# Loading q and k by 256 tokens in an attention and SwiGLU kernel on one Trainium2 core

## The chip, the cores and the metric

The kernel runs on one core of one Trainium2 chip. A core has five engines that run side by side, each working through its own list of instructions in order: TensorE (PE in the profile, with its weight loads as PEld), VectorE (DVE), ScalarE (ACT), GpSimd (POOL) and SyncE (SP). POOL and SP do no arithmetic here: they issue DMA transfers, which 16 DMA engines carry out. An instruction that waits for a semaphore holds up everything behind it on its own engine. The metric is device time in microseconds (us), the median of several runs.

## The reference

Inputs are q, k and v (8 batches, 8 heads, 576 tokens, 64 values a head, float32) and three weight matrices. The first half is causal attention over a sliding window of 128 tokens with an ALiBi bias, a slope for each head:

```python
scores = scale * np.matmul(q, k.transpose(0, 1, 3, 2))
rel = pos[:, None] - pos[None, :]
bias = slopes[:, None, None] * (-np.abs(rel).astype(np.float32))[None, :, :]
mask = (rel >= 0) & (rel < window)
scores = np.where(mask, scores + bias[None], -1000000000.0)
# softmax over the keys, then
np.matmul(attn, v)
```

Its output, 4608 tokens of 512 values, goes through a SwiGLU block without biases:

```python
g = x @ w_gate
silu = g * (1.0 / (1.0 + np.exp(-g)))
val = x @ w_val
return (silu * val @ w_out).astype(np.float32)
```

with 512 inputs, 1536 hidden values and 512 outputs.

## The kernel before

**Attention.** Two batches make a super-batch, and the 36 units of attention are 9 tiles of 128 tokens in each of 4 super-batches: four tiles of its first batch, four of its second, and one tile made of the last 64 tokens of both. Such a tile of q, k or v is called a rank, 0 to 35. For a unit, `scores` multiplies a rank's transposed k with the transposed q of this and the next rank (line 289; line 325 for a batch's last tiles), ACT takes the exponential (295, 329), DVE multiplies by a mask that holds the exponentials of the bias (301, 333), `weighted` multiplies by V with a column of ones beside it (357), and DVE divides by that column (360, 361). The result x is transposed into xT (385 to 389, for late units by a DMA, 379).

**Loading q, k and v.** POOL issues all loads from HBM that turn float32 into float16, in an order written out by hand at lines 917 to 955 and by `loads_to` afterwards, seven ranks ahead. A load of q or k (line 188) brings one rank as 128 tokens, 8 heads and 64 values: 1024 runs of 256 bytes in HBM, 128 bytes in SBUF. At most eight of POOL's loads are under way: each waits for the one eight places earlier.

**Transposing q and k.** Scores need both with the 64 values on the partitions. Ranks below `QK_DMA_FROM` = 11 are transposed by PE, four instructions a tile (215), and copied out of PSUM by DVE (220) or ACT (218). Later ranks are transposed by a DMA that SP issues (236), four units ahead (`ahead`). They land in `kT` and `qT`, rings of 12 and 9 ranks.

**The feed-forward part.** Tokens are taken in nine blocks of 512. For each of 12 slices of 128 hidden values, PE computes pg = w_gate·xT and pv = w_val·xT (413); ACT takes tanh into tt (431), DVE makes uu = (tt + 1)·pg (432) and hT = uu·pv (443). Three PSUM buffers called gv go round among pg and pv; for the first two slices of the first block four buffers of the other pool are used, the one that transposes and scores take too. Output projections follow (467 and, with seven products in place of eight, 548 to 590). Blocks 6 to 8 do the gate and value products by sevens as well (637). SP issues the stores (459), in line with its transposes.

**What sets the order.** The start, up to unit 4, and the first steps of `ffn` are written out in order for PE, DVE and ACT (`tc.manual_schedule`). In between, `everything` interleaves steps of `ffn` with steps of `attention` by a target count, and the framework's scheduler lays out the engines from a model of costs; from step 60 the order of PE is as written. On the chip each engine follows that fixed order.

Of the kernel before, what the change touches and what calls it, by code (L numbers as in the profile page):

```python
# [10 lines left out]
FP32 = mybir.dt.float32  # L11
# [5 lines left out]
P = 128  # L17
WIN = 128
QK_DMA_FROM = 11
X_DMA_FROM = 22  # L20
MASKS_AT = (3.0, 5.0, 6.0, 7.0)
# [22 lines left out]
def make_distance():  # L44

    u = np.arange(2 * P)[None, :] - np.arange(P)[:, None]
    return np.where((u >= 0) & (u < WIN), u, 16000).astype(np.float32)
# [3 lines left out]
def kernel(  # L51
# [25 lines left out]
    dist, idf = stage[:, 5, 0:256], stage[:, 5, 256:384]  # L77
    hw = {key: stage[:, n] for n, key in enumerate((("k", 0), ("q", 0)))}
# [9 lines left out]
    dist_d = nc.inline_tensor(make_distance(), name="distance")  # L88
    nc.scalar.dma_start(dist, dist_d.ap())

# [11 lines left out]
    def later_masks():  # L102
        for h in by_slot:
            nc.scalar.activation(reg[:, slot(h), :], dist, AF.Exp, scale=-(2.0 ** (-8.0 * (h + 1) / H)))


    NK, NQ = 12, 9
# [11 lines left out]

    def make_mask(n):  # L120
        to, of = ((msk[0][:, :, 0:64], reg[:, :, 128:192]),
                  (msk[1][:, :, 64:128], reg[:, :, 128:192]),
                  (msk[2][0:64, :, 0:64], reg[0:64, :, 0:64]),
                  (msk[2][64:128, :, 64:128], reg[64:128, :, 64:128]))[n]
        nc.scalar.copy(to, of)
# [8 lines left out]
    nat = ctx.enter_context(tc.tile_pool(name="nat", bufs=5))  # L134
# [16 lines left out]
    VROW = 80  # L151
# [7 lines left out]


    units = [(s, p) for s in range(NSUP) for p in range(9)]
    last = len(units) - 1
    NR = 9 * NSUP

    natq, natk, va = {}, {}, {}

    def transposed_home(name, rank):
        return kT[:, rank % NK] if name == "k" else qT[:, rank % NQ]

    def source(src, rank):  # L170

        s, c = divmod(rank, 9)
        if c == 8:
            return [((64 * n, 64 * n + 64),
                     src[2 * s + n, :, 512:576, :].rearrange("h p d -> p h d")) for n in range(2)]
        b, t = 2 * s + c // 4, c % 4
        return [((0, P), src[b, :, t * P:(t + 1) * P, :].rearrange("h p d -> p h d"))]

    def load_v(rank):
        va[rank] = va_all[rank % NV]  # L180
        for (p0, p1), src in source(v, rank):
            nc.gpsimd.dma_start(va[rank][p0:p1, :, 0:D], src)  # L182

    def load_qk(rank, which="kq"):
        for name in which:
            t_ = nat.tile([P, H, D], FP16, name=name + "n", tag=name + "n")
            for (p0, p1), src in source(k if name == "k" else q, rank):
                nc.gpsimd.dma_start(t_[p0:p1], src)  # L188
            (natk if name == "k" else natq)[rank] = t_

    def load(rank):
        load_qk(rank)
        load_v(rank)

    def transposed(name, rank):

        if rank < FIRST:
            pt = ps_f.tile([P, 4, P], FP32 if (name, rank) in hw else FP16, name="pt",
                           tag="gv" if name == "k" or rank == 1 else "po",
                           bufs=3 if name == "k" or rank == 1 else 1)  # L200
        else:
            pt = ps_a.tile([P, 4, P], FP16, name="pt", tag="a")
        if (name, rank) in hw:

            for _ in range(IDLE[(name, rank)]):
                nc.tensor.matmul(pt.rearrange("p j t -> p (j t)"), idle[:, 0:P], idle,
                                 start=True, stop=True)
            for j in range(4):
                nc.tensor.transpose(pt[:, j, :], hw[(name, rank)][:, j * P:(j + 1) * P], idf)
            nc.vector.tensor_copy(transposed_home(name, rank), pt)  # L210
            return
        t_ = (natk if name == "k" else natq).pop(rank)

        for j in range(4):
            nc.tensor.transpose(pt[:, j, :], t_[:, 2 * j:2 * j + 2, :],
                                idm if rank < FIRST else idm2)
        if name == "k" and rank >= FIRST:
            nc.scalar.copy(transposed_home(name, rank), pt)
        else:
            nc.vector.tensor_copy(transposed_home(name, rank), pt)  # L220


    order = []
    for s in range(NSUP):
        for half in (0, 4):
            order += [(name, 9 * s + half + r) for name, r in zip("kqqkqkqk", (0, 0, 1, 1, 2, 2, 3, 3))]
        order += [("k", 9 * s + 8), ("q", 9 * s + 8)]
    need = [18 * s + n for s in range(NSUP) for n in (3, 5, 7, 8, 11, 13, 15, 18 if s else 16, 18)]

    def transpose(n):  # L230
        name, rank = order[n]
        if rank < QK_DMA_FROM:
            transposed(name, rank)
            return
        t_ = (natk if name == "k" else natq).pop(rank)
        nc.sync.dma_start_transpose(transposed_home(name, rank), t_.rearrange("p h d -> p (h d)"))
# [98 lines left out]
    xs = {}  # L335

    def weighted(i):
# [4 lines left out]
        for half in range(2):  # L342
# [15 lines left out]
            rec = xpool.tile([P, 4, 1], FP32, name="rec", tag="rec", bufs=4)  # L358
            with tc.high_priority() if i in (6, 7) else ExitStack():
                nc.vector.reciprocal(rec, av[:, :, D:D + 1])  # L360
                nc.vector.tensor_mul(x[:, 4 * half:4 * half + 4, :], av[:, :, 0:D],  # L361
                                     rec.broadcast_to([P, 4, D]))
# [89 lines left out]
    def rows_of(n, j):  # L452
        if n == 8:
            return [(0, 64, 2 * j * S + 512), (64, 128, (2 * j + 1) * S + 512)]
        return [(0, 128, n * S + j * P)]

    def store(n, j, osb, c0=0, c1=512, two=False):
        for i, (p0, p1, r0) in enumerate(rows_of(n, j)):
            (nc.scalar if two and i else nc.sync).dma_start(out[r0:r0 + p1 - p0, c0:c1],
                                                            osb[p0:p1, c0:c1])  # L460
# [17 lines left out]
    HM = NMB // 2  # L478
    HC = DM // 2
    T1, T2, T3, T4 = (consts.tile([P, HM, HC], FP16, name=f"T{n}") for n in (1, 2, 3, 4))  # L480
# [124 lines left out]
    t_homes = [halves(kT[:, n]) for n in range(NK)] + [halves(qT[:, n]) for n in range(NQ)] + spare[6:9]  # L605

    def gate_val_weight_sums(u):

        cols = slice(2 * u * P, (2 * u + 2) * P)
        t1, t2, t3, t4 = tsum[u] = t_homes[4 * u:4 * u + 4]  # L610
        return [lambda: nc.vector.tensor_sub(t1, V1[:, :, cols], G1[:, :, cols]),
                lambda: nc.vector.tensor_sub(t3, V2[:, :, cols], V1[:, :, cols]),
                lambda: nc.vector.tensor_sub(t2, V2[:, :, cols], t1),
                lambda: nc.vector.tensor_sub(t4, G2[:, :, cols], t2)]
# [191 lines left out]
    loaded = done_t = 0  # L806

    def loads_to(r):
        nonlocal loaded
        while loaded <= min(r, NR - 1):  # L810
            load(loaded)
            loaded += 1

    def transposes_to(n):
        nonlocal done_t
        while done_t < n:
            transpose(done_t)
            done_t += 1

    def ahead(i):  # L820

        n = need[min(i + 4, last)]
        while done_t < n and order[done_t][1] < loaded and order[done_t][1] >= QK_DMA_FROM:
            transposes_to(done_t + 1)
# [13 lines left out]
    def first_tiles():  # L838

        first_masks()  # L840
        transposes_to(1)
        begin_scores(0, 0, 0)
        transposes_to(2)
        begin_scores(0, 0, 1)
        transposes_to(need[0])
# [3 lines left out]
        for n, _ in enumerate(run(scores(0))):  # L849
            if n == 0:  # L850
                begin_scores(1, 0, 1, ps_f, "gv", 3)
                transposes_to(need[1])
        for i in range(FIRST):
            if i + 1 < FIRST:
                for n, _ in enumerate(run(scores(i + 1))):
# [3 lines left out]
                    if n == 0 and i + 2 < FIRST:  # L859
                        transposes_to(need[i + 2])  # L860
# [12 lines left out]
    def attention():  # L873

        waiting = []
        transposes_to(need[FIRST])
        for _ in run(scores(FIRST)):
            yield FIRST
        for i in range(FIRST, last + 1):
            late = i >= LATE  # L880
            if i < last:
                transposes_to(need[i + 1])
# [8 lines left out]
            loads_to(i + 7)  # L891
            ahead(i)
# [24 lines left out]
    load_qk(1, "qk")  # L917
    load_qk(2, "q")
    load_v(0)
    load_qk(2, "k")  # L920
    load_qk(3, "q")
    load_v(1)
    load_qk(3, "k")
# [5 lines left out]
    load_qk(4)  # L929
    load_qk(5, "q")  # L930
    load_w(512, 640, "v")
    load_w(640, 768, "v")
    load_w(768, 1024, "g")
    load_qk(5, "k")
    load_qk(6, "q")
# [3 lines left out]
    load_qk(6, "k")  # L939
    load_qk(7, "q")  # L940
    load_v(5)
    load_w(1280, 1536)
    load_qk(7, "k")
    load_v(6)
    load_qk(8)
    load_wo(8, 12)
    load_v(7)
    load_wo(4, 8)
    load_qk(9)
    load_qk(10, "q")  # L950
    load_wo(0, 4)
    load_v(8)
    load_v(9)
    load_qk(10, "k")
# [16 lines left out]
    def attention_ends():  # L971
        while att_step():
            pass
        of = supool.tile([P, 1], FP16, name="turn", tag="turn", bufs=1)
        nc.scalar.activation(of, ex[(NSUP - 1, "c", 2)][:, 0, 0:1], AF.Silu)
# [74 lines left out]
```

## Time and profile before

| what | value |
|---|---|
| three runs | 335.38, 336.21, 337.46 us; median 336.21 |
| span of the profiled execution, first to last instruction | 333.9 us |
| TensorE busy | 325.9 us, 98% |
| VectorE busy | 274.2 us, 82% |
| ScalarE busy | 206.9 us, 62% |
| POOL busy issuing DMAs | 111.0 us, 33% |
| packets of POOL's queue | 118880, 18.62 MB |
| packets of SP's queue | 42064, 17.90 MB |

The profile gives the span of the profiled execution and no separate time for it; the span is 2.3 us under the median of the three runs. Busy shares are means over the whole span. A matmul is shown with its whole latency and matmuls overlap, so PE can be shown as busy while it starts less than it could. The times of DMA packets overlap too.

### The profile page before, as it was taken

To read this page: it belongs to the slowest core of one execution; us is meant where nothing else is said; L and a number is where in the kernel's file an instruction comes from. 1 tells how busy PE (TensorE), PEld (TensorE's weight loads), DVE (VectorE), ACT (ScalarE), POOL (GpSimd) and SP (SyncE) were. 2 spreads that over 40 slices of the span, in tenths; PEclk is the share of its full clock that TensorE was granted. 3 is DMA by queue.
4 is the path that set the end of the run, shared out by engine and by line. 5 is a ranking of instruction groups with operands and counts; after the bars stand their busy time and mean duration, and the time that the engine had idled before them with its cause. 6 is when DMAs were issued, how large, how long until landed. Compare 5 with 4: busy or idle time off the path is not lost.

```text
span 333.9 us, 7719 instructions
## 1 busy us (share of the span) xinstructions
PE 325.9 (98%) x2955; PEld 218.5 (65%) x2955; DVE 274.2 (82%) x643; ACT 206.9 (62%) x413; POOL 111.0 (33%) x138
## 2 busy tenths in 40 slices
PE   8999999999999999999999999999999999999994
PEld 4665465544465655656655655666788888888883
DVE  4678878999797879988999999999855985775683
ACT  4976777464766657567456465563567667776650
POOL 8977776458964098551035000000000000000000
PEclk9999999999999999999999999999999999999999
DMA  9999999999999999999969532030100101011014
GB/s 154 175 179 175 177 185 164 122 142 184 141 170 159 140 195 162 160 168 155 179 128 152 117 34 81 16 96 17 65 29 36 64 2 65 25 41 65 0 65 127
DMA packets 161669, 37.64 MB, mean 113 GB/s; under 512 B 149472, under 2 KB 157280, under 8 KB 161632
## 3 DMA queue, kind: packets, MB, share of 16 engines
q0 software_dynamic: 118880, 18.62, 78.8%
q1 hardware_dynamic: 42064, 17.90, 27.8%
q10 hardware_dynamic: 688, 0.62, 0.6%
q8 instruction: 23, 0.38, 0.5%
q14 instruction: 14, 0.11, 0.1%
HBM read 37.91 MB, written 9.44 MB: 142 GB/s over the span
## 4 chain that ended last, share of the span: by engine, by line
PE 87%; DVE 8%; ACT 2%; issue 1%; DVEq 0%
PE po L548 19%; PE pg L413 17%; PE pv L413 16%; PE gX L637 9%; PE av L357 5%; PE gY L637 5%; PE ps L289 3%; PE p L548 3%; PE gZ L637 2%; DVE uu L432 2%; PE psc L325 2%; DVE hT L443 2%; PE po L467 2%; PE px L385 2%; DVE ex L301 1%
## 5 line engine op out<-in xcount | busy, mean ns | idle before, releaser
L413 PE MATMUL pv<-xT,wv_sb 128*128 128x512 f16 (+2 forms) x312 | 76.6, 363 | 0.3 <-DVE uu L432 0.2
L413 PE MATMUL pg<-xT,wg_sb 128*128 128x512 f16 (+2 forms) x324 | 76.5, 355 | 0.1
L431 ACT ACTIVATE tt<-pg 128x512 f16<-128x512 f32 x68 | 40.9, 603 | 44.6 <-PE pg L413 44.6
L295 ACT ACTIVATE ex<-ps 128x512 f16<-128x512 f32 x96 | 50.0, 608 | 7.4 <-PE ps L289 7.4
L432 DVE SCALAR_TENSOR_TENSOR uu<-tt,pg 128x512 f16<-128x512 f16 x67 | 45.6, 681 | 8.6 <-ACT tt L431 8.3
L443 DVE TENSOR_TENSOR hT<-uu,pv 128x512 f16<-128x512 f16 x68 | 46.2, 681 | 1.6
L182 POOL DMA_DIRECT2D va<-in_v_dram x40 | 34.5, 871 | 38.2 <-DMA out_dram<-osb 20.4
L548 PEld LDWEIGHTS <-hT 128*128 128x128 f16 x384 | 37.2, 98 | 10.7 <-issue 0.8
L413 PEld LDWEIGHTS <-wg_sb 128*128 128x128 f16 x324 | 28.5, 98 | 23.5 <-issue 2.2
L413 PEld LDWEIGHTS <-wv_sb 128*128 128x128 f16 x312 | 27.8, 98 | 24.4 <-issue 2.3
L188 POOL DMA_DIRECT2D kn<-in_k_dram x39 | 33.5, 863 | 18.8 <-DMA qT<-qn 6.2
L188 POOL DMA_DIRECT2D qn<-in_q_dram x39 | 33.6, 871 | 9.7 <-DMA va<-in_v_dram 4.7
L548 PEld LDWEIGHTS <-S 128*128 128x128 f16 x288 | 27.5, 98 | 7.5 <-issue 1.4
L301 DVE TENSOR_TENSOR ex<-ex,m_reg 128x1024 f16<-128x1024 f16 x42 | 28.5, 685 | 3.0 <-ACT ex L295 3.0
L361 DVE TENSOR_TENSOR x<-av,rec 128x256 f16<-128x256 f32 x72 | 28.5, 420 | 0.5
L548 PE MATMUL po<-T,S 128*128 128x256 f16 x192 | 25.9, 273 | 0.3 <-ACT u2s L574 0.3
L548 PE MATMUL po<-T,hT 128*128 128x256 f16 x192 | 26.0, 272 | 0.0
L329 ACT ACTIVATE exc<-psc 128x512 f16<-128x512 f32 x40 | 21.4, 608 | 3.2 <-PE psc L325 3.1
L691 DVE TENSOR_TENSOR hT<-s,v 128x512 f16<-128x512 f16 x18 | 7.6, 424 | 17.7 <-ACT s L690 17.7
L357 PEld LDWEIGHTS <-ex 128*128 128x128 f16 x384 | 17.5, 98 | 4.4 <-issue 1.0
L357 PE MATMUL av<-va,ex 128*128 128x65 f16 x384 | 19.3, 193 | 0.3 <-ACT ex L295 0.3
L289 PE MATMUL ps<-qT,kT 64*128 64x256 f16 x192 | 16.0, 272 | 0.9 <-DVE qT L220 0.6
(129 smaller groups left out, 534.1 us busy)
## 6 DMA issues: line engine op xcount, KB each, us to landing
out_dram<-osb SPq DMA_DIRECT2D x32, 256.0 KB, 2.4
va<-in_v_dram POOLq DMA_DIRECT2D x32, 128.0 KB, 6.9
qn<-in_q_dram POOLq DMA_DIRECT2D x31, 128.0 KB, 7.9
kn<-in_k_dram POOLq DMA_DIRECT2D x31, 128.0 KB, 7.3
wg_sb<-in_moe_w_gate_dram POOLq DMA_DIRECT2D x6, 256.0 KB, 7.6
wo_sb<-in_moe_w_out_dram POOLq DMA_DIRECT2D x3, 512.0 KB, 8.2
wv_sb<-in_moe_w_val_dram POOLq DMA_DIRECT2D x5, 256.0 KB, 7.6
kn<-in_k_dram POOLq DMA_DIRECT2D x8, 64.0 KB, 6.4
```

Of the source, the lines that this page charges most:

```text
L182: nc.gpsimd.dma_start(va[rank][p0:p1, :, 0:D], src)
L188: nc.gpsimd.dma_start(t_[p0:p1], src)
L295: nc.scalar.activation(e[:, o:o + 2, :], banks[q4][par], AF.Exp, scale=scale)
L301: nc.vector.tensor_mul(e[:, o, :], e[:, o, :], reg[:, o, :])
L357: nc.tensor.matmul(av[:, j, :], w, val, start=(n == 0), stop=(n == len(todo) - 1))
L361: nc.vector.tensor_mul(x[:, 4 * half:4 * half + 4, :], av[:, :, 0:D], rec.broadcast_to([P, 4, D]))
L413: nc.tensor.matmul(ps[:, c0:c1], w[:, kb, ms], xT[n][:, kb, c0:c1], start=(kb == 0 and c0 == 0), stop=(kb == NKB - 1 and c1 == 512), skip_ ...
L431: nc.scalar.activation(tt, pg[:, c0:c1], AF.Tanh, scale=0.5)
L432: nc.vector.scalar_tensor_tensor(out=uu, in0=tt, scalar=one if (n, m) == PIN else 1.0, in1=pg[:, c0:c1], op0=ALU.add, op1=ALU.mult)
L443: nc.vector.tensor_mul(hT[n][:, m, c0:c1], acted[(n, m)][1][:, c0:c1], pv[:, c0:c1])
L548: nc.tensor.matmul(dst, a[:, m, cols], b[:, m, :], start=(start and m == 0), stop=(m == HM - 1), skip_group_check=True)
L637: nc.tensor.matmul(dst[:, i, :], w[:, kb, c0 + i * P:c0 + (i + 1) * P], a[:, kb, :], start=(start and i == 0 and kb == 0), stop=(i == 1 an ...
```

## The change

Of q and k, batch 0 and the 64-token tails are loaded as before (`load_small`). For batches 1 to 7 one load brings 256 tokens, partition p holding tokens 2p and 2p + 1 (`load_raw`): 1024 runs of 512 bytes in HBM, 256 bytes in SBUF. `sort` then puts the two tokens apart by two copies on DVE, 128 partitions by 512 values of float16 each. In batch 1 PE transposes the sorted tiles (`spread`). From rank 9 on a DMA does: the first 64 partitions of a sorted tile give one rank, the last 64 the other, with the even tokens ahead of the odd ones in each (`by_dma`). V, the masks and the stores follow that order of tokens; for V and the stores this takes two DMAs of 64 partitions in place of one of 128. The masks come from a second distance table, loaded by ACT. `kT` keeps 10 ranks, the rows of V are 65 values apart and no more 80, three buffers each hold loaded and sorted halves, and the sorts are placed some units ahead (`SORT_AHEAD`, `AHEAD`). `issue_after` holds a sort behind the division of the unit it names on DVE.

```diff
-QK_DMA_FROM = 11
+AHEAD = 3
+SORT_AHEAD = 4
+RAW, BY = 3, 3
...
+RUN = 2
...
+def make_distance(run):
+    j = np.arange(P)
+    t = run * (j % (P // run)) + j // (P // run)
+    u = np.concatenate([t, P + t])[None, :] - t[:, None]
     return np.where((u >= 0) & (u < WIN), u, 16000).astype(np.float32)
...
+    dist_s_d = nc.inline_tensor(make_distance(RUN), name="distance_spread")
+    nc.scalar.dma_start(dist_s, dist_s_d.ap())
...
-    NK, NQ = 12, 9
+    NK, NQ = 10, 9
...
-    VROW = 80
+    VROW = D + 1
...
+    def load_raw(name, half):
+        b, g = half
+        n = 2 * DM
+        at = (2 * (name == "q") + g) * n
+        t_ = (nat.tile([P, n], FP16, name=name + "raw", tag="raw", bufs=RAW) if b > 1
+              else t_all[:, at:at + n])
+        raw[name, half] = t_.rearrange("p (h t d) -> p h t d", h=H, t=RUN)
+        src = of_input(name)[b, :, 256 * g:256 * g + 256, :].rearrange("h (p t) d -> p h (t d)", p=P)
+        nc.gpsimd.dma_start(raw[name, half].rearrange("p h t d -> p h (t d)"), src)
...
+        run = RUN if b else 1
+        src = v[b, :, c * P:(c + 1) * P, :].rearrange("h (p t) d -> t p h d", t=run)
+        for t, n in enumerate(range(0, P, P // run)):
+            nc.gpsimd.dma_start(va[rank][n:n + P // run, :, 0:D], src[t])
...
+    def sort(name, half):
+        t_ = nat.tile([P, 2 * DM], FP16, name=name + "by", tag="by", bufs=BY)
+        t_ = by_token[name, half] = t_.rearrange("p (j t c) -> p j t c", j=4, t=RUN)
+        for t in range(RUN):
+            nc.vector.tensor_copy(t_[:, :, t, :].rearrange("p j (e d) -> p j e d", e=2),
+                                  raw[name, half][:, :, t, :].rearrange("p (j e) d -> p j e d", e=2))
+
+    def spread(name, n):
+        g, t = divmod(n, RUN)
+        if t == 0:
+            with tc.issue_after(divided[FIRST - 1].ins):
+                sort(name, (1, g))
+        pt = ps_a.tile([P, 4, P], FP16, name="pt", tag="a")
+        for j in range(4):
+            nc.tensor.transpose(pt[:, j, :], by_token[name, (1, g)][:, j, t, :], idm2)
+        w = P // RUN
+        to = (kT if name == "k" else qT)[:, 4 + RUN * g:4 + RUN * g + RUN, :, w * t:w * t + w]
+        (nc.scalar.copy if name == "k" else nc.vector.tensor_copy)(
+            to.rearrange("p c j q -> p j c q"), pt.rearrange("p j (c q) -> p j c q", c=RUN))
+
+    def by_dma(name, rank):
+        to, c = home(name, rank), rank % 9
+        if c == 8:
+            nc.sync.dma_start_transpose(to, nat_of.pop((name, rank)).rearrange("p h d -> p (h d)"))
+            return
+        half, r0 = (2 * (rank // 9) + c // 4, c % 4 // 2), P // RUN * (c % 2)
+        nc.sync.dma_start_transpose(
+            to.rearrange("p j (t q) -> p (j t) q", t=RUN),
+            by_token[name, half][r0:r0 + P // RUN].rearrange("p j t c -> p (j t c)"))
...
-        return [(0, 128, n * S + j * P)]
+        w = P // RUN
+        return [(w * t, w * t + w, n * S + j * P + t, RUN) for t in range(RUN)]
...
+    def sort_at(which):
+        name, (b, g) = which
+        return max(6, first_rank(b) + 2 * g - SORT_AHEAD + (name == "k"))
+
+    def loads_at(i):
+        while loaded <= min(i + 7, last):
+            load_v(loaded)
+            loaded += 1
+        while sorted_ < len(raw_order) and i >= sort_at(raw_order[sorted_]):
+            with tc.issue_after(divided[i].ins):
+                sort(*raw_order[sorted_])
+            sorted_ += 1
+            if sorted_ + RAW <= len(raw_order):
+                load_raw(*raw_order[sorted_ + RAW - 1])
...
-            loads_to(i + 7)
-            ahead(i)
+            loads_at(i)
+            if i == 9:
+                make_mask(4)
+            transpose_dma(dma_need[min(i + AHEAD, last)])
...
     load_w(512, 768, "g")
-    load_qk(4)
-    load_qk(5, "q")
-    load_w(512, 640, "v")
-    load_w(640, 768, "v")
+    load_raw("q", (1, 0))
+    load_raw("k", (1, 0))
+    load_w(512, 768, "v")
+    load_raw("q", (1, 1))
+    load_raw("k", (1, 1))
     load_w(768, 1024, "g")
```

In the built program the scheduler has put the first three sorts on DVE as follows: after the third of the four copies of line 387 stands the sort of q's first half of batch 1, then the fourth copy of line 387, then the sorts of k's first half and q's second half, and then the first uu of line 432. PE has 16 transposes fewer (ranks 9 and 10 of q and k); apart from the stretch between units 4 and 12 its order is as before. The 24 later sorts follow, one or two to a unit, the divisions of units 6 to 30; the sort of a half's k, whose first rank is r, stands behind the division of unit r − 3 (for r = 9, of unit 6).

## Prediction

> **What bounds the kernel now.** I read the busy shares first, then the table by stretches of 10 us, to see where an engine has nothing left to give, then the timelines of DVE, PE and POOL around the place where the first sorts are put.
>
> The first line of the page, and three stretches (length; busy us and instructions of PE, PEld, DVE, ACT and POOL; granted clock; DMA share; GB/s):
>
> ```profile
> PE 325.9 (98%) x2955; PEld 218.5 (65%) x2955; DVE 274.2 (82%) x643; ACT 206.9 (62%) x413; POOL 111.0 (33%) x138
> ...
> 20.00:30.00 10.00, 9.93 (x72) 5.10 (x70) 8.42 (x15) 7.84 (x16) 8.36 (x11) 1.00 1.89 178
> ...
> 100.00:110.00 10.00, 9.75 (x113) 6.31 (x108) 7.81 (x17) 6.71 (x14) 3.79 (x5) 1.00 1.85 159
> ...
> 160.00:170.00 10.00, 10.00 (x89) 5.64 (x88) 10.00 (x27) 5.36 (x12) 0.00 (x0) 1.00 0.81 154
> ```
>
> PE sets the time: the page's chain of waits gives it 87% of the span, and any time that it stands still is added to the end. No transfer shows among its waits, so a quicker load gains nothing by itself. DVE has some 10.7 us free between 80 and 160, and 0.5 between 160 and 200. What has to be found is where the change makes PE wait.
>
> DVE's timeline at the start of the feed-forward part (start us, us):
>
> ```profile
> 18.19 0.41 DVE L387 COPY xT<-px 128x512 f16<-128x512 f16 x1
> 18.97 0.42 DVE L387 COPY xT<-px 128x512 f16<-128x512 f16 x1 [0.37 <-PE px L385]
> 20.72 0.69 DVE L432 SCALAR_TENSOR_TENSOR uu<-tt,pg 128x512 f16<-128x512 f16 x1 [1.32 <-ACT tt L431]
> 21.52 0.69 DVE L443 TENSOR_TENSOR hT<-uu,pv 128x512 f16<-128x512 f16 x1
> 22.12 0.68 DVE L432 SCALAR_TENSOR_TENSOR uu<-tt,pg 128x512 f16<-128x512 f16 x1
> 22.91 0.69 DVE L443 TENSOR_TENSOR hT<-uu,pv 128x512 f16<-128x512 f16 x1
> 23.51 0.68 DVE L432 SCALAR_TENSOR_TENSOR uu<-tt,pg 128x512 f16<-128x512 f16 x1
> ```
>
> and PE's:
>
> ```profile
> 19.67 0.39 PE L413 MATMUL pg<-xT,wg_sb 128*128 128x128 f16 x4
> ...
> 23.15 1.03 PE L413 MATMUL pv<-xT,wv_sb 128*128 128x512 f16 x4
> 24.25 1.02 PE L413 MATMUL pg<-xT,wg_sb 128*128 128x512 f16 x4
> ```
>
> The pg at 24.25 writes the gv buffer that the third uu (23.51 + 0.68 = 24.19) has just read; four such matmuls take 0.86 us, so the pv of 23.15 was through at 24.01 and PE stood still for 0.24. There is no reserve: what delays the first uu delays PE by as much. Likewise the matmuls at 19.67 need the last copy of line 387 (done at 19.39).
>
> POOL's timeline, with the loads in question:
>
> ```profile
> 12.97 0.88 POOL L909 DMA_DIRECT2D wg_sb<-in_moe_w_gate_dram  x1
> 13.71 1.02 POOL L188 DMA_DIRECT2D kn<-in_k_dram  x1
> 14.58 1.89 POOL L188 DMA_DIRECT2D qn<-in_q_dram  x2
> 16.31 1.66 POOL L909 DMA_DIRECT2D wv_sb<-in_moe_w_val_dram  x2
> ```
>
> These are issued far ahead of landing. By the trace's landing events the queue serves them one after the other: the wg of 12.97 lands at 21.21, the k at 22.09, the two q at 22.93 and 23.76, the two halves of wv at 24.50 and 25.25. A load of 1024 packets of 128 bytes thus costs the queue 0.85 us, 512 packets of 256 bytes 0.74, 512 packets of 512 bytes 1.33 (19.88 to 21.21).
>
> **The change, part by part.**
>
> *The first sorts.* They stand on DVE ahead of the fourth copy of line 387 and the first uu, and wait for the raw loads that now follow that wg: q, k, wv, q. A raw load is 1024 packets of 256 bytes, so 2 x 0.74 = 1.47 us; the ends are 1.33 (the weight load of equal bytes) and 1.70 (two loads of k). I take 1.47, whose packets are the same size. Landings: first q 21.21 + 1.47 = 22.68, k 24.15, wv 25.48, second q 26.95 (26.5 to 27.6). No such copy is in the trace; the nearest rows are 0.27 (memset of 256 words) and 0.59 (the cast of line 98), I take 0.30. The fourth copy of line 387 then runs at 22.68 + 0.6 = 23.3 in place of 18.97, and PE, which has nothing else it may do, stands from 19.7 to about 23.8. The first uu runs at 26.95 + 0.6 = 27.55 in place of 20.72: **+6.8 us** (6.4 to 8.1). ACT, PE and the eight-fold queue of loads wait behind it in step, and PE is at its limit afterwards, so the loss stays.
>
> *Start.* ACT issues one more table of 128 KB beside the first loads; the one before lands 3.1 us after its issue, and it shares the DMA engines with the tiles that the first transposes wait for: +0.3 (0 to 0.5).
>
> *PE.* 16 transposes of 128 columns fewer, 0.055 us each in the run from 19.67 on (four in 0.22): -0.9. The copies of ranks 9 and 10 out of PSUM go too (2 on DVE, 2 on ACT), against two new mask instructions on ACT's free time: 0.
>
> *DMA load.* 28 raw loads at 1.47 replace 56 at 0.85: 6.4 us of queue time. Nothing on PE waits for it, so 0. [...] By the rows the gain per byte is 13%.
>
> *Transposes by DMA.* The sort of a half's k stands after the division of unit r - 3 (6 for r = 9); then SP issues its transpose, and scores(r) waits for the landing. Laid out at 0.86 us for four 512-column matmuls, the work that PE has between the weighted products of that unit and scores(r) is 6.0 us for r = 9, 4.4 for 13, 6.8 for 15, 7.5 for 31, 8.1 for 22 and 8.3 to 9.6 for the others. Needed: about 1.3 for the division, 0.6 for the sort, and the landing:
>
> ```profile
> kT<-kn SPq DMA_TRANSPOSE x25, 6.3
> ```
>
> With 6.3 it is 8.2, so PE waits 2.2 + 3.8 + 1.4 + 0.1 = 7.5; with 5.0 it is 3.5. A transpose of 64 partitions by 1024 moves the bytes of one of 128 by 512; not shown before, its landing is bounded by 2.4 (xT<-x) and 8.9 (the slowest kT or qT), which makes 0 and some 20. Since the queue is a little shorter I take **+5**; the 6.3 row is the nearest. SP's extra issues for stores (0.33 to 0.53 us each) fall into its idle time.
>
> *The other copies.* 24 sorts are 48 copies of 0.3. 17 sorts fall before 160 and use about 10 us of free time. Seven (4.2 us) fall between 160 and 200, where 0.5 is free; weight sums that DVE runs at 176 to 190 (lines 611 to 614) are wanted by PE only after 237 and can give way. I take +1 (0 to 4.6).
>
> *V.* Twice as many DMAs of half the size, rows 65 values apart: 0, with loads far ahead of use; if the packets get slower, the four early V loads move the hole by some tenths.
>
> [...]
>
> **Sum.** 333.9 + 6.8 + 0.3 - 0.9 + 5 + 1 = 346.1 for the span; the median stands 2.3 above the profiled span, so **348 us**.
>
> **The rivals.**
> 1. Only the hole at the start counts: transposes land in time and the copies hide. 333.9 + 6.8 + 0.3 - 0.9 + 2.3 = 342.4. For it: before, transposes have landings near 4 and 5 us at 60 to 80. Against: 4.4 us for rank 13. Chance 0.20.
> 2. Everything costs its upper end: copies of 0.59, 64-partition transposes with double issue time on SP (2.4 in place of 1.2). Some 9 more: 357. Against: the bytes are the same. Chance 0.15.
> 3. The other side, not slower: the hole is paid back. From 28 to 60 the chain of waits has 27.5% outside PE on its larger DVE, ACT and issue lines (8.8 us). If late DVE lets ACT and the loads run ahead and these waits vanish, 342.4 - 8.8 = 333.6; it decides from a payback of 2.8 on. Against: they are ACT-to-DVE-to-PE sequences whose length doesn't shrink when all start later. Chance 0.07.
> 4. The sorts don't hold DVE because the loads are there, so that the change is only fewer transposes: 335.3. It takes four loads by 20.7, where the queue is not through the weights. Chance 0.03.
>
> My forecast has 0.55. The range 340 to 358 leaves out the two last and the edges. One percent is about what can be told from no change here: faster 0.03, within 0.08, slower 0.89.
>
> **What would show it.** In the profile after, DVE idle before the sorts at 19 to 27 us, ended by a DMA; first uu near 27.5; PE's busy share down in 20 to 30; waits of scores for DMA transposes near ranks 9, 13 and 15; DVE still near 10 in 160 to 200. The forecast fails if the second raw q lands before 24, or if PE's stretch from 28 to 60 gets shorter by more than 3 us.

## The result and the profile after

The changed kernel takes **376.19 us** (median of 4 runs, 373.44 to 376.83) against 335.79 (4 runs, 335.37 to 337.46) on the same chip: a ratio of 1.117, 95% interval 1.112 to 1.122. The span of its profiled execution is 374.2 us, 40.3 more than before. The forecast of 348 (340 to 358) had the direction and less than a third of the size. Of the runs below, one of early_raw, one of tails and two of v_later are over 1.5% longer than the fastest of their kernel, at a lower granted clock (0.963 beside 0.976, 0.971 beside 0.981, 0.952 and 0.945 beside 0.963); the medians take in all four runs, the ratios leave these out, and v_later has no ratio.

The first line of the page, and from its part on the chain of waits the shares of the span by engine:

```profile
PE 335.9 (90%) x2939; PEld 221.5 (59%) x2939; DVE 285.7 (76%) x697; ACT 207.6 (55%) x412; POOL 99.8 (27%) x137
...
PE 58%; DVE 16%; DMA 15%; ACT 3%; POOL 3%; issue 3%; POOLq 0%
```

The same shares before:

```profile
PE 87%; DVE 8%; ACT 2%; issue 1%; DVEq 0%
```

PE was 98% busy and 87% of the chain; now it is 90% and 58%, and transfers, which had no share, have 15%. PE's list of waits (what PE waited for: us in total, times, longest) names them:

```profile
PE ps L377 <- DMA qT<-qby: 13.5, 4, 7.2
PE ps L377 <- DMA kT<-kby: 12.6, 6, 4.2
PE pg L501 <- DVE xT L475: 4.1, 1, 4.1
```

Ten waits of the scores for DMA transposes, 26.1 us together, and the hole at the start, 4.1. In the kernel before the same list holds no transfer, and its longest entry is 1.2 us in the warm-up:

```profile
PE nil L148 <- DVE kT L111: 1.2, 1, 1.2
PE ps L289 <- DVE qT L220: 0.6, 2, 0.4
```

The stretches of 10 us in which most of the wait falls (columns as in the prediction):

```profile
20.00:30.00 10.00, 5.88 (x28) 3.22 (x27) 3.70 (x10) 3.58 (x7) 5.30 (x8) 0.66 1.67 187
60.00:70.00 10.00, 4.83 (x25) 2.51 (x26) 2.64 (x4) 3.20 (x6) 5.38 (x7) 0.53 2.09 115
100.00:110.00 10.00, 5.92 (x55) 2.91 (x54) 6.42 (x17) 4.33 (x9) 7.63 (x12) 1.00 1.67 127
110.00:120.00 10.00, 5.75 (x40) 2.81 (x39) 5.13 (x12) 5.05 (x11) 1.21 (x2) 0.93 1.52 150
160.00:170.00 10.00, 8.23 (x84) 5.01 (x82) 9.15 (x26) 4.29 (x9) 7.23 (x10) 1.00 1.52 136
170.00:180.00 10.00, 5.76 (x32) 2.67 (x30) 5.09 (x11) 3.74 (x7) 3.61 (x5) 0.83 1.90 133
```

In five of these six PE is idle for four to five tenths, and in four the granted clock (the third number from the end; 1.00 in every such stretch of before but the last) has fallen: there a long wait is followed by matmuls at half speed (behind the hole four of 512 columns take 1.71 us, from 25.79 to 27.50, in place of 0.86).

**Where 40.3 us come from.** I counted, from the starts of all matmuls, by how much each start lies behind the time that the matmul before it needs (0.213 us for 512 columns, half of the 0.427 from start to start at half clock; at full clock the median is 0.216). The sum is 16.8 us before and 57.9 after, 41.1 more; 16 transposes fewer give 0.9 back. The 41.1 consist of the hole (4.3 by this count), the scores that wait for transposes (27.7: rank 9 7.3, 13 2.6, 14 1.7, 15 4.4, 22 1.7, 23 4.4, 27 2.2, 28 0.7, 29 0.5, 31 2.0), and some 9 that are nearly all half clock: the clock stands at 0.50 for about 21.5 us in which PE works, which is worth at most 10.8.

**The hole at the start**, in DVE's timeline:

```profile
18.38 0.42 DVE L475 COPY xT<-px 128x512 f16<-128x512 f16 x1
23.25 0.50 DVE L280 COPY qby<-T 128x512 f16<-128x512 f16 x2 [4.46 <-DMA T<-in_q_dram]
23.66 0.42 DVE L475 COPY xT<-px 128x512 f16<-128x512 f16 x1
24.69 0.49 DVE L280 COPY kby<-T 128x512 f16<-128x512 f16 x2 [0.60 <-DMA T<-in_k_dram]
27.50 0.49 DVE L280 COPY qby<-T 128x512 f16<-128x512 f16 x2 [2.32 <-DMA T<-in_q_dram]
27.91 0.68 DVE L520 SCALAR_TENSOR_TENSOR uu<-tt,pg 128x512 f16<-128x512 f16 x1
```

DVE waits in turn for three raw loads; the copy of line 475 that PE needs runs at 23.66 (forecast 23.3), the first uu at 27.91 (forecast 27.55; 20.72 before).

**A late transpose**, rank 13. DVE's timeline, then SP's, then PE's:

```profile
96.87 0.42 DVE L449 TENSOR_TENSOR x<-av,rec 128x256 f16<-128x256 f32 x1
97.21 0.48 DVE L280 COPY kby<-kraw 128x512 f16<-128x512 f16 x2
```

```profile
97.76 2.51 SPq L304 DMA_TRANSPOSE kT<-kby  x2
```

```profile
99.21 0.81 PE L558 MATMUL po<-wo_sb,hT 128*128 128x512 f16 x3
102.46 0.39 PE L377 MATMUL ps<-qT,kT 64*128 64x256 f16 x4 [2.44 <-DMA kT<-kby]
```

The last division of unit 10 ends at 97.2, the sort follows at once, SP issues at 97.76, the tile lands at 102.41 by the trace's landing events, and PE, out of other work at 99.9 by the starts of its matmuls, starts at 102.46. Before, the k of rank 13 was issued at 66.1 and landed at 72.0, for scores at 83.2 (SP's timeline and PE's of the kernel before):

```profile
66.13 1.19 SPq L236 DMA_TRANSPOSE kT<-kn  x1
83.25 0.39 PE L289 MATMUL ps<-qT,kT 64*128 64x256 f16 x4
```

The three times of rank 22 were 107.1, 115.7 and 137.2, and are now 160.5, 165.1 and 165.2. The medians of the landing hardly moved:

```profile
qT<-qby SPq DMA_TRANSPOSE x24, 6.7
kT<-kby SPq DMA_TRANSPOSE x24, 6.6
```

Before they were 6.3 for kT and 6.8 for qT. At the median the transfers did not become slow; they lost their lead of ten to twenty microseconds. The first six, of ranks 9 to 12, did: issued between 52 and 61 with seven or eight of POOL's loads in flight, they landed in 7.3 to 10.6, where the four that the kernel before issued between 57 and 62, with one to five in flight, took 2.5 to 4.9.

### The profile page after: what moved, and what is told of

It is laid out like the page before. It is cut to its first block, busy times and chain, and to the rows that moved or that the text cites. A ratio compares the mean times of both kernels' runs of the same rounds, so it can differ in the third digit from the quotient of the medians.

```text
span 374.2 us, 7761 instructions
## 1 busy us (share of the span) xinstructions
PE 335.9 (90%) x2939; PEld 221.5 (59%) x2939; DVE 285.7 (76%) x697; ACT 207.6 (55%) x412; POOL 99.8 (27%) x137
## 4 chain that ended last, share of the span: by engine, by line
PE 58%; DVE 16%; DMA 15%; ACT 3%; POOL 3%; issue 3%; POOLq 0%
PE po L638 14%; PE pv L501 10%; PE pg L501 10%; PE gX L729 8%; DMA kT<-kby 6%; DMA qT<-qby 6%; PE gY L729 4%; DVE uu L520 3%; DMA T<-in_q_dram 3%; PE p L638 2%; DVE hT L531 2%; PE ps L377 2%; PE gZ L729 2%; PE av L445 2%; DVE x L449 2%
## 5 line engine op out<-in xcount | busy, mean ns | idle before, releaser
L501 PE MATMUL pg<-xT,wg_sb 128*128 128x512 f16 (+2 forms) x324 | 79.2, 367 | 4.1 <-DVE xT L475 4.1
L501 PE MATMUL pv<-xT,wv_sb 128*128 128x512 f16 (+2 forms) x312 | 80.4, 379 | 0.0
L240 POOL DMA_DIRECT2D va<-in_v_dram x60 | 42.1, 712 | 29.3 <-PE av L445 19.1
L531 DVE TENSOR_TENSOR hT<-uu,pv 128x512 f16<-128x512 f16 x68 | 46.2, 680 | 3.7 <-PE pv L501 2.6
L501 PEld LDWEIGHTS <-wg_sb 128*128 128x128 f16 x324 | 29.7, 102 | 29.1 <-issue 8.5
L501 PEld LDWEIGHTS <-wv_sb 128*128 128x128 f16 x312 | 28.9, 102 | 25.7 <-issue 5.9
L638 PEld LDWEIGHTS <-hT 128*128 128x128 f16 x384 | 37.4, 99 | 11.2 <-issue 0.8
L377 PEld LDWEIGHTS <-kT 64*128 64x128 f16 x192 | 8.0, 95 | 37.8 <-issue 19.7
L227 POOL DMA_DIRECT2D kraw<-in_k_dram x12 | 10.8, 898 | 52.4 <-DVE qby L280 50.9
```

What stands on the lines that cost most here:

```text
L240: nc.gpsimd.dma_start(va[rank][n:n + P // run, :, 0:D], src[t])
L377: nc.tensor.matmul(two[par][:, j, :], kT[rows, ks, pair, :], qT[rows, p:p + 2, pair, :], start=(j == 0 and not early_tile), stop=(j == 1))
L501: nc.tensor.matmul(ps[:, c0:c1], w[:, kb, ms], xT[n][:, kb, c0:c1], start=(kb == 0 and c0 == 0), stop=(kb == NKB - 1 and c1 == 512), skip_ ...
L531: nc.vector.tensor_mul(hT[n][:, m, c0:c1], acted[(n, m)][1][:, c0:c1], pv[:, c0:c1])
L638: nc.tensor.matmul(dst, a[:, m, cols], b[:, m, :], start=(start and m == 0), stop=(m == HM - 1), skip_group_check=True)
```

## The experiments

Each kernel below is the changed one with the edit shown. Medians are of four runs, beside runs of the kernel before with medians of 335.79 to 336.34. Span and waits are those of the profiled run.

| kernel | median us | ratio to before, 95% | span | PE's waits for kT, qT by DMA |
|---|---|---|---|---|
| changed | 376.19 | 1.112 to 1.122 | 374.2 | 26.1 (10) |
| no_hole | 373.38 | 1.107 to 1.115 | 371.6 | 21.1 (9) |
| unit_earlier | 355.33 | 1.054 to 1.061 | 354.3 | 8.3 (3) |
| tails | 366.41 | 1.081 to 1.094 | 367.0 | 19.6 (7) |
| early_raw | 374.97 | 1.107 to 1.119 | 371.8 | 23.7 (9) |
| v_later | 382.19 (377.7 to 384.0) | not given | 378.6 | 29.5 (9) |
| together | 350.97 | 1.041 to 1.045 | 348.6 | 2.5 (2) |
| together_pe9 | 348.05 | 1.031 to 1.036 | 345.8 | 1.7 (1) |
| tails_ring4 | 364.13 | 1.076 to 1.091 | 362.6 | 16.3 (7) |
| mended | 346.79 | 1.024 to 1.035 | 345.1 | 1.9 (1) |
| mended_r | 355.84 | 1.051 to 1.061 | 353.9 | 9.2 (3) |

### unit_earlier: the same transfers, called for sooner

```diff
-        return max(6, first_rank(b) + 2 * g - SORT_AHEAD + (name == "k"))
+        return max(6, first_rank(b) + 2 * g - SORT_AHEAD + (name == "k") - 1 * (b > 2))
...
-            transpose_dma(dma_need[min(i + AHEAD, last)])
+            transpose_dma(dma_need[min(i + AHEAD + 1 * (i > 7), last)])
```

> From batch 3 on every sort is held behind the division one unit earlier, and the transposes by DMA are called for one unit earlier; same copies, same transfers, same buffers. Theory A (the placing is what is late): the waits of scores for landings at ranks 13, 14, 15, 22, 23, 27, 28, 29 and 31 (20.2 us of idle PE) nearly go, with some 2 to 3 us of half clock behind them: span 350 to 354. The wait ahead of scores(9) stays at 7.3. Rival B (the transfers are what is late: DMA engines and queues have no more to give): transposes issued earlier land later by as much, the median landing of 6.6 grows to 9 or more, and less than half of the gain comes: 363 or more.

355.33: 20.9 us less. The two longest of PE's waits:

```profile
PE ps L377 <- DMA qT<-qby: 8.1, 2, 7.6
PE pg L501 <- DVE xT L475: 4.2, 1, 4.2
```

Of ten waits for transposes one of size is left, at rank 9, whose sorts were not moved. The median landings even grew a little, to 7.4 and 7.1. So half of the loss is the placing of the sorts behind the division of unit r - 4 or r - 3, with that of the transposes called after them: shown, and rival B is out.

### tails: what stands ahead on SP

```diff
-            nc.sync.dma_start_transpose(to, nat_of.pop((name, rank)).rearrange("p h d -> p (h d)"))
+            with tc.issue_after(turned[-1].ins):
+                nc.sync.dma_start_transpose(to, nat_of.pop((name, rank)).rearrange("p h d -> p (h d)"))
...
```

(`turned` collects the transposes of line 304.)

> The transposes of the 64-token tails (line 301) are held behind the last transpose of the super-batch's other ranks on SyncE; nothing else is changed. Theory A (SyncE's order is a part of the lateness): in the changed kernel SyncE issues the tails' kT and qT ahead of kT of rank 15, qT of 24 and kT of 31, and waits for their loads first; without that rank 15 lands 3.3 us earlier, 24 some 4, 31 1.3: span about 8 to 9 us less with the clock that follows, 365. Rival B (SyncE's order does not matter, sorts and transfers set the time): no change, 373 to 375.

366.41 (363.1 to 369.2), 9.8 less; the profile is of the longest run. In the changed kernel SP's timeline has the tails' transposes, which must wait for their own loads, between the q and the k of ranks 15 and 16:

```profile
101.27 2.57 SPq L304 DMA_TRANSPOSE qT<-qby  x2
106.17 2.03 SPq L301 DMA_TRANSPOSE kT<-kn  x1
108.37 1.28 SPq L301 DMA_TRANSPOSE qT<-qn  x1
109.75 0.57 SPq L550 DMA_DIRECT2D out_dram<-osb  x1
110.43 2.80 SPq L304 DMA_TRANSPOSE kT<-kby  x2
```

The k of rank 15 had been sorted by 107.1 and was issued at 110.43. SP's order is a part of the lateness, as theory A had it; without the longest run the median is 365.0, 11.2 less. These gains overlap with the 20.9 of unit_earlier, which left no wait of size behind the tails either, and are not to be added to it.

### no_hole: the hole taken away

```diff
-            with tc.issue_after(divided[FIRST - 1].ins):
+            with tc.issue_after(valued[-1].ins):
```

(`valued` collects the instructions that write hT, so that the sorts of batch 1 stand behind the fourth one.)

> The four sorts of batch 1 are held behind the fourth hT of block 0 on VectorE in place of the last division of the start; nothing else is changed. Theory A (the hole at the start is a loss that stays): VectorE no longer waits for raw loads ahead of the first uu, which runs near 20.7 again; the idle of PE ahead of 24.13 (4.3 us) and the stretch at half clock that follows it (2.2 us of matmul starts) go, so the span falls by 6.5 to about 367.7. Rival B (paid back at rank 9): the raw q and k of half (2,0) and the q of (2,1) land by POOL's queue at 48.3, 50.3 and 58.9 whatever PE does, and the transposes of rank 9 and 10 come behind these; scores(9) then starts only some 2.5 us earlier than 65.2 and the wait ahead of it grows from 7.3 to about 11: span about 371.7.

373.38: 2.8 less, and the two intervals overlap. The hole is gone, and other waits stand in its place; DVE's timeline and PE's:

```profile
48.67 0.49 DVE L280 COPY qby<-qraw 128x512 f16<-128x512 f16 x2 [2.27 <-DMA qraw<-in_q_dram]
50.21 0.62 DVE L280 COPY kby<-kraw 128x512 f16<-128x512 f16 x2 [1.04 <-DMA kraw<-in_k_dram]
```

```profile
51.22 1.04 PE L413 MATMUL psc<-qT,kT 64*128 64x128 f16 x16 [3.82 <-DVE qT L271]
```

The sorts for rank 9 now come before their raw loads have landed (48.65 and 50.2, by POOL's queue, whatever PE does), DVE waits for them, and PE for DVE; scores(9) waits another 3.1. Rival B was right in the span (371.6 for 371.7) and in that the gain goes at rank 9; the waits there are 6.9, part of them on DVE, and not 11.

### early_raw and v_later: rank 9

Raw loads of half (2,0) ahead of the first load of w_out, and sorts from unit 5:

```diff
+    load_raw("q", (2, 0))
+    load_raw("k", (2, 0))
     load_wo(8, 12)
-    load_raw("q", (2, 0))
+    load_raw("q", (2, 1))
     load_v(7)
-    load_raw("k", (2, 0))
     load_wo(4, 8)
     load_v(8)
     load_wo(0, 4)
-    load_raw("q", (2, 1))
...
-        return max(6, first_rank(b) + 2 * g - SORT_AHEAD + (name == "k"))
+        return max(5, first_rank(b) + 2 * g - SORT_AHEAD + (name == "k"))
```

> The raw loads of q and k of half (2,0) and of q of (2,1) stand ahead of, or between, the first two loads of w_out in POOL's queue, and the sorts of half (2,0) may run from unit 5 on; nothing else is changed. Theory A (rank 9 is late because its raw loads and its transposes stand in a queue of 8 loads): the raws land near 43, 45 and 49, the transposes of ranks 9 and 10 are issued some 4 to 6 us earlier, the wait ahead of scores(9) shrinks from 7.3 to 1 to 3, and the 5.7 us at half clock behind it go: span 365 to 368. Rival B (the landing of 9.7 us is what counts, and issuing earlier lands no earlier since the V loads fill the engines): scores(9) starts at 64 or later, span 373 to 374.

374.97, not told apart from the changed kernel. The raws landed at 44.1, 46.2 and 51.9, and the transposes for rank 9 were issued at 50.1, 51.7 and 53.1 in place of 52.7, 54.1 and 55.4; they landed at 59.0, 61.9 and 63.5 (before the edit 60.0, 62.4, 65.0), and scores(9) started at 63.5.

V loaded four ranks ahead:

```diff
-        while loaded <= min(i + 7, last):
+        while loaded <= min(i + 4, last):
```

> After the loads that are written out, V is loaded four ranks ahead in place of seven; nothing else is changed. Theory A (the transposes of ranks 9 and 10 stand behind the loads that POOL issued before them): with the V loads of ranks 11 to 14 gone from the stretch of 50 to 66, the q of rank 10 (issued 55.4, landed 65.0) lands 3 to 5 us earlier and the wait ahead of scores(9) falls from 7.3 to 3 or 4; with the half clock behind it the span is 368 to 371, unless V itself becomes late. Rival B (the time goes into the placing alone, what else is in the queue does not matter): scores(9) starts at 64.5 or later, span 373 to 375.

377.7 to 384.0, slower: the two shorter runs, 377.7 and 380.4, are above all four of the changed kernel. Raw loads came up into the place of the V loads, the q of rank 10 landed at 65.2, and the k that scores waits for at 234.8 came 5.5 us late. Theory A failed in both: scores(9) started at 63.5 and 65.3, against 65.2 in the changed kernel. What they have in common: in this stretch seven or eight loads are in flight whenever a transpose is issued, and the transpose lands in 8.0 to 10.9 us (7.3 to 10.6 in the changed kernel). That these loads are the cause I did not isolate, and why rank 9 waits is open to that extent.

### together and together_pe9

The edits of no_hole, unit_earlier and the load order of early_raw in one (sorts of half (2,0) from unit 6, as in the changed kernel); then `spread` for half (2,0) too, so that PE transposes ranks 9 and 10:

```diff
-    pe_order += [("k", 8), ("q", 8)]
+    pe_order += [("k", 8), ("q", 8)] + [(n, t) for n in ("Q", "K") for t in (4, 5)]
-    pe_need = [3, 5, 7, 8, 12, 16, 16, 16, 18]
+    pe_need = [3, 5, 7, 8, 12, 16, 16, 16, 18, 22]
...
```

> no_hole, unit_earlier and the load order of early_raw in one kernel (sorts of half (2,0) behind unit 6 as in the changed kernel). Theory A (the hole at the start is paid back only because the raws of half (2,0) land too late for it, and the late placing is a separate loss): now the hole's 6.5 us come through as far as the raws at 44, 46 and 52 allow, with 20 us from the placing; the wait at scores(9) stays at 6 to 8 with its clock: span 344 to 350. Rival B (the transposes at 50 to 65 land when the queue allows, whatever is done before): scores(9) still starts near 63.5 and the span is 352 or more.

> together, with PE instead of a DMA transposing ranks 9 and 10 (16 transposes of 128 columns and eight copies out of PSUM more). Theory A (what is left at rank 9 is the landing of its transposes): the wait ahead of scores(9) goes, and the first landings that count are those for rank 11; with 0.9 us of PE work more the span is 335 to 339, which is the kernel before within 1 or 2%. Rival B (what is left at rank 9 is the raw loads and the sorts): the sorts of 52 still end late, PE waits ahead of the transposes in place of scores(9), and the span is 343 or more.

350.97 and 348.05. Beside the right placing, the hole and the load order are worth 4.4 (355.33 to 350.97). The span of together, 348.6, is in theory A's range. together_pe9, at 345.8, missed its 335 to 339. Part of it is a wait for V; PE's timeline:

```profile
53.89 0.23 PE L452 MATMUL av<-va,exc 128*128 128x65 f16 x1 [3.29 <-DMA va<-in_v_dram]
```

The new load order had pushed the V of rank 7 behind the raws.

### mended, tails_ring4 and mended_r

mended is together_pe9 with that V and the next ahead of w_out. tails_ring4 is tails, and mended_r is mended, with a fourth raw buffer, since in the changed kernel each sort sets free a load of 256 KB that POOL issues beside the transposes: the sort at 97.21 is followed by the transposes at 97.76 and a raw load at 97.99. The order of loads in mended, and the edit of the other two:

```diff
+    load_raw("q", (2, 0))
+    load_v(7)
+    load_raw("k", (2, 0))
+    load_v(8)
     load_wo(8, 12)
-    load_raw("q", (2, 0))
-    load_v(7)
-    load_raw("k", (2, 0))
+    load_raw("q", (2, 1))
     load_wo(4, 8)
-    load_v(8)
+    load_v(9)
     load_wo(0, 4)
-    load_raw("q", (2, 1))
-    load_v(9)
     load_v(10)
...
-RAW, BY = 3, 3
+RAW, BY, RAW_BUFS = 3, 3, 4
-    opool = ctx.enter_context(tc.tile_pool(name="op", bufs=7))
+    opool = ctx.enter_context(tc.tile_pool(name="op", bufs=6))
```

(The tiles tagged `raw` have RAW_BUFS buffers; loads are still called for RAW ahead.)

> together_pe9 with V of rank 7 and 8 ahead of the loads of w_out and the raws of half (2,0) between them: hole closed, sorts a unit earlier, ranks 9 and 10 transposed by PE. Theory A (what was left in together_pe9 is V of rank 7, behind which PE stood for 3.5 us at 50.4, and the clock after it): both go, span 339 to 342. Rival B (the queue as a whole is too late by then: another load takes the place of V): another wait of 2 to 4 us at 45 to 65, span 344 to 347.

> The kernel of the run tails, with four raw buffers in place of three while raw loads are still called for three ahead, so that a raw load waits for the sort before last and no longer for the sort just done; six output buffers in place of seven make the room. The order of every engine and queue is that of tails. Theory A (a sort sets free a load of 256 KB that POOL issues 0.2 us after the first transpose of its pair, and the transposes land beside or behind it): the first transposes of a pair land in 2.5 to 3.5 us in place of 4.5 to 4.8 from rank 13 on, the second ones in 3 to 5 in place of 6.5 to 7; the waits of scores at 13, 15, 22, 23 and 27 shrink by 2 to 4 each: 356 to 361 where tails had 366.4. Rival B (the transposes land in 6.6 whatever loads are beside them, or the loads only move to another transpose): no change, 364 to 368.

> mended with four raw buffers as in tails_ring4 (six output buffers). Theory A: the waits for landings that are left in mended after 100 (1 to 3 us in all) go as well, span 1 to 3 below mended, 337 to 340, which is the kernel before plus 1%. Rival B: six output buffers or the order of the tails on SyncE cost as much as is won, the same as mended within 1.

mended: 346.79, only 1.3 less than together_pe9. V was no longer waited for; other waits stood there, 1.9 us at 49.0 (DVE waits for the raw k) and 1.9 at 157.9 (the k of rank 24, behind a tail on SP):

```profile
PE ps L384 <- DMA kT<-kby: 1.9, 1, 1.9
PE psc L420 <- DVE qT L271: 1.9, 1, 1.9
```

Rival B's span (344 to 347, measured 345.1) came true, and how much of together_pe9's miss was V's stays open. tails_ring4: 364.13 against 366.41, with overlapping ranges and the same median landings (6.5 and 6.7): rival B. The fourth buffer did not free the transposes of loads beside them; 42 of the 54 were issued with some in flight, 47 in tails. mended_r was 9 us slower than mended. PE, DVE, ACT and POOL have the same order in both; on SP the tails moved ahead of the q of rank 15. SP's list of waits in mended_r between 80 and 106, and PE's timeline:

```profile
SPq L307 <- DMA kn<-in_k_dram: 9.8, 2, 9.3
```

```profile
103.66 1.04 PE L384 MATMUL ps<-qT,kT 64*128 64x256 f16 x8 [8.38 <-DMA qT<-qby]
```

The q of rank 15 had been sorted at 87.0 in mended_r; SP stood 9.3 us before a tail whose load had not landed, issued the q at 95.83, and PE waited 8.4 for it. In mended the same q was issued at 86.2 and landed at 93.1, without a wait. It is the clearest price of SP's order in these runs; rival B had named the order of the tails, but with a loss no larger than the gain. What a fourth buffer alone is worth in mended stays unknown.

No version beat the kernel before. One with mended's edits and the tails held back was not run, so how near the changed loading can come stays open; 11 us of mended's span remain over before: some 4 in the two waits named, and at most some 4 at the lower clock, by the mean granted clock of 0.988 over its span of 345.1; the rest I did not trace.

## Why the prediction was wrong

- **The first sorts** (+6.8): right in mechanism, place and time, 27.91 against 27.55 for the first uu. At its place it cost 4.3 of idle and some 2 at half clock. That "the loss stays" was wrong as long as the raws of half (2,0) land when they do: taken away alone it gave 2.8. The rival "paid back" had 0.07; what pays is not a shorter chain, as it supposed, but a later wait for loads that PE doesn't move.
- **Start** (+0.3), **PE** (-0.9), **DMA load** (0): small and about as taken. The scores of the fourth unit start at 15.06 us against 14.87, 0.2 later; 16 transposes are gone; a raw load took 1.44 (the weights ahead of the first q landed at 21.79, the q at 23.23), near the 1.47 assumed.
- **Transposes by DMA** (+5, 0 to 20): this is the step that failed; the term measured 27.7, and half clock came on top. The chain was named rightly, "the sort of a half's k stands after the division of unit r - 3", and the landing was right at the median. But the work beside it was compared with that k alone and with nothing ahead of it on SP. Three things were missed. Scores also wait for the second transpose of a pair and for the q of the next rank: rank 9 waited for the third transpose in line (issued 55.35, landed 65.03), rank 14 for the q of 15, 23 for that of 24. On SP the tails, waiting for loads of their own, stood ahead of rank 15 and 24. And in places the landing was 7 to 10.6, not 6.3. By the step rank 9 would wait 2.2 and waited 7.3, 13 3.8 and 2.6, 15 1.4 and 4.4, 22 0.1 and 1.7; the ranks set at nothing, 14, 23 and 27 to 29, waited 9.5. Rank 31, with 7.5 of work against 8.2 needed, is missing from the sum (0.7; measured 2.0). The upper end was worked out short as well: with a landing of 8.9, 10.8 are needed, which makes 21 for the five ranks named and 8 or more for the others, so some 30 and not 20. unit_earlier took away all but rank 9's and 0.5 at one later place. "SP's extra issues fall into its idle time" was the wrong question: an engine that waits is idle in the sums, and yet holds up what is behind it (SP in mended_r for 9.3 us).
- **The clock** was no term at all. Behind the waits the granted clock stands at 0.50, and matmuls of 512 columns start 0.427 us apart in place of 0.216, some 9 us in all. The trace before has nothing of the kind: no wait of PE is above 1.2 us, and the clock is 1.00 as long as PE works. In the changed kernel the fall comes some 3 us into the hole of 4.1 us that the prediction itself laid out: 0.50 from 23.0 to 29.8.
- **The other copies** (+1): 0.286 us at the median, as taken (0.30); two of 56 took 0.50 to 0.53, both beside a POOL issue. Twelve copies ran beside a POOL issue, ten of them in 0.27 to 0.30, so an issue beside them cost nothing to speak of here.
- **V** (0): no wait for V in the changed kernel.
- **Rival 2** had the upper end of the landing, but put it down to slow issues and copies of 0.59; SP's issues took 1.3, the copies 0.29. The range ended at 358 because the upper end of the transposes (some 20) was never added to the likeliest sum.

## What to carry to other kernels

When an operation is put between a load and its use, count the lead of the last transfer, not its duration: find the instruction that the new step waits for, and add from there the sort, everything ahead in the issuing queue (with what that waits for), the longest landing in that stretch, and compare it with the work that the consumer has left, for each operand and not for the first alone. In the kernel before, the k of ranks 13 and 22, issued 17 and 30 us ahead of use, hid all of this; one tied to a recent result hid only what the consumer's other work covered (rank 13 in the changed kernel: PE out of other work at 99.9, the landing at 102.41). And a wait that is taken away at one place gains only up to the next thing that has its own time, here POOL's loads (in no_hole raw loads that landed at 48.65 and 50.2).

## What the hardware showed

In the changed kernel the granted clock falls to 0.50 at 23.0, 60.5, 118.6, 176.6 and 231.2 us, and comes back 6.8, 10.2, 3.4, 3.4 and 3.4 later. In this trace the falls are 37.55, 58.03, 58.03 and 54.61 us apart, which is 11, 17, 17 and 16 times 3.413, the length of the shortest of these stretches. At 118.6 PE had been running again for 0.6 us when the clock fell. 1.9 us of idle (228.7 to 230.6) were followed by a fall at 231.2, while 2.6 us (99.9 to 102.5) were followed by none. What made the difference is not shown. So, in this one run, a wait of some 2 us cost either its own length or, by an estimate from the 1.9 and half of the 3.4 us at half clock behind it, nearly twice that.

How long a DMA transpose takes to land goes with the loads that POOL has in flight when it is issued. In the changed kernel the median of kT and qT is 2.8 us with none in flight, 6.4 with one or two, 7.9 with seven or eight (5.7 to 10.6); in the kernel before it is 3.5 with one or two (five transposes) and 7.2 with seven or eight. One or two loads go with a longer landing than before; raw loads are now twice as large (256 KB in place of 128) and are issued beside the sort, but that this is the cause is not shown: the fourth raw buffer, which was to part them, did not shorten the landing (6.5 and 6.7 us at the median, as in tails).
